# Segment attention on one core: one stretch of 64-row tiles, sums of half 0 in column tiles, value chunks in quarters, dense row copies

## The chip, the core and the metric

One core of a Trainium2 chip runs the whole program. The metric is the device time of one execution in microseconds (us), the median of several runs. Engines are named as in the profile: PE is TensorE (matmul), PEld its weight loads, DVE is VectorE, ACT ScalarE, POOL GpSimd, SP SyncE.

## What is computed

Four layers with residual sums: A, B, A, B, each on the layer norm of the 2048 x 512 input. B is a gated MLP with a 2048 x 2048 spatial matmul and takes little of the time. A is attention with a recurrent memory, and its recurrence sets the order of everything:

```python
B, S, Dm = (1, 2048, 512); H, Dh = (32, 128); M, seg = (8, 32)
mem = mem0
for s in range(n_seg):                                # 64 segments of 32 rows
    h = concatenate([mem, x[:, s * 32:(s + 1) * 32]])  # 8 memory rows + 32 rows
    q, k, v = h @ Wq, h @ Wk, h @ Wv                   # 32 heads of 128
    p = softmax(where(mask, q @ k.T * scale, -1e9))    # 40 x 40 for each head
    o = (p @ v) @ Wo
    mem = o[:, :8]                                     # input of the next segment
    outs.append(o[:, 8:])
```

## The kernel before

**Blocks.** `a_block` runs layer A, `b_block` layer B, each twice. In `a_block` a loop over 64 segments calls `segment`; the order of PE, DVE and ACT is the order in which the program issues them (`manual_schedule`), while the queues of POOL and SP are ordered by the framework. The 32 heads are worked in two halves `r` (0 and 1) of 16 heads.

**Two sorts of rows.** The 32 rows of a segment that it computes at once (24 new rows and the 8 memory rows that the segment before has just made) are `hT`, 32 columns wide. The projections of the last 8 rows of the four segments of a block of 128 rows don't hang on the memory: they are computed ahead for the whole block, by `b_units` (tiles `psb`), and the output projection of such rows is made afterwards, by `y_part` (tiles `pwB`). Both are generators, and `fill()` issues their next few matmuls; a segment calls it three times and gets 4, 8 and 20 matmuls. These matmuls are what PE does while the chain of a segment is in another engine. Some segments have nothing left to fill with.

**A segment, as PE sees it.** `qk(0)`, `qk(2)`, `qk(1)`, `qk(3)` are the chunks of Q (0, 1) and K (2, 3), `v_mm(0)` and `v_mm(1)` those of V: 16 matmuls each (`mm_chunk`, L710: 4 steps `kt` over the 512 input columns, times 4 column tiles of 32 columns, so a chunk of 32 rows fills all 128 partitions). `qk` copies its chunk from PSUM to a bf16 tile `rows` (L920), and `qk_T` turns it with DVE's 32 x 32 transpose into QQ or KA (L923). The element order in `rows` interleaves two heads, so that the transpose can move pairs as one 4-byte word. `scores(r)` are 20 small matmuls (L946, L950) into `psS`; `exps(r)` is their exponential (L955), `close(r)` multiplies by the mask and makes E (L958). E stands in a layout in which the keys of two heads lie in the 64-row halves of the partitions; so what reads E as the moving operand uses tiles of 64 rows and 128 columns: `sums_memory(r)` (L972, the denominators of the memory queries, by a matrix of ones), `pv(r)` (L989, L992, E times V, where `VA` is the copied value chunk, L1034 and L1043), and `sums_tokens` (L981, all other denominators).

**The way out.** `memory_out(r)` turns the denominators into reciprocals (logarithm and exponential on ACT, L1006 and L1007) and writes the 8 memory rows of `uT` (L1008). `wo_pairs` and `wo_rest` (L790, L797) project them with Wo; `fold` and `build_hA` add the parts and transpose the new memory into the next segment's `hT` (L895), which its first `qk` waits for. `tok_out` and `last_out` (L1011, L1014) write the other rows with the reciprocals of `sums_tokens` (L1076, L1079).

**DVE's tail.** After `last_out(1)` DVE runs what is left for the end of a segment: in some segments an addition of finished outputs (L826, or L832 for a first copy), in some a normalisation for layer B (`y_norm`, L245). The next segment's transposes queue behind it.

**PSUM.** `att` holds psQ, then psS, then psT; `attO[0]` psK, then psO[0]; `attO[1]` psO[1]; `accA` and `accB` take turns for chunks, fill and px. `other_bank` tells the framework that two accesses to a tile lie in different banks.

Of the kernel before, what the change touches and what calls it, by code (L numbers as in the profile page):

```python
# [7 lines left out]
BF16 = mybir.dt.bfloat16  # L8
F32 = mybir.dt.float32
ACT = mybir.ActivationFunctionType  # L10
ALU = mybir.AluOpType
# [3 lines left out]
P = 128  # L15
# [48 lines left out]
def _consts(ctx, tc, c, b_sp):  # L64
    nc = tc.nc
    cp = ctx.enter_context(tc.tile_pool(name="consts", bufs=1))
    bsp = cp.tile([P, 16], F32, name="bsp")
    tctx = ExitStack()
    tmp = tctx.enter_context(tc.tile_pool(name="consts_tmp", bufs=1))
    maskf = tmp.tile([P, 224], F32, name="maskf")  # L70
    nc.gpsimd.memset(maskf[:], 1.0)
    fourth = tmp.tile([P, 4, 32], F32, name="fourth")
    nc.gpsimd.memset(fourth[:], 0.0)
    nc.gpsimd.affine_select(out=fourth[:], in_=fourth[:], compare_op=ALU.not_equal, fill=1.0,
                            base=0, pattern=[[-1, 4], [-4, 32]], channel_multiplier=1)
    own = maskf[:, 160:224].rearrange("p (i q) -> p i q", i=4)
    is_own = tmp.tile([P, 4, 1], F32, name="is_own")
    nc.vector.tensor_reduce(out=is_own[:], in_=fourth[:], op=ALU.max, axis=mybir.AxisListType.X)
    nc.vector.tensor_copy(own, is_own[:].to_broadcast([P, 4, 16]))
    for q in range(0, P, 32):  # L80
        blk = maskf[q:q + 32, 0:160].rearrange("p (i q) -> p i q", i=4)[:, :, 8:32]
        nc.gpsimd.affine_select(out=blk, in_=blk, compare_op=ALU.is_ge, fill=0.0, base=8,
                                pattern=[[0, 4], [1, 24]], channel_multiplier=-1)
        last = own[q:q + 32, :, 8:16]
        nc.gpsimd.affine_select(out=last, in_=last, compare_op=ALU.is_ge, fill=0.0, base=0,
                                pattern=[[1, 4], [4, 8]], channel_multiplier=-1)
    maskN = cp.tile([P, 2, 224], BF16, name="maskN")
    nc.vector.memset(maskN[:], 0.0)
    for gs in range(4):
        nc.vector.tensor_copy(maskN[32 * gs:32 * gs + 32, gs % 2, :], maskf[32 * gs:32 * gs + 32, :])  # L90
    ones = cp.tile([P, P], BF16, name="ones")
    nc.vector.memset(ones[:], 1.0)
    bsp_bf = cp.tile([P, 16], BF16, name="bsp_bf")

    def load_bsp():
        nc.vector.memset(bsp_bf[:], 0.0)
        nc.sync.dma_start(bsp_bf[:], b_sp.rearrange("(t p) -> p t", p=P))
        return lambda: nc.vector.tensor_copy(bsp[:], bsp_bf[:])

    c["bsp"], c["load_bsp"] = bsp, load_bsp  # L100
    tctx.close()
    c.update(maskN=maskN, ones=ones)
    return c


# [476 lines left out]
def cols_rhs(w, j, kt, cg):  # L582
    at = 2048 * (j % 2) + 512 * cg
    return w[j // 2][:, kt, at:at + 512]
# [81 lines left out]
def a_block(tc, c, rows, front, MV_in, RS_in, MV_out, RS_out, ahead, wo, S, first):  # L666
# [1 line left out]
    NSEG = S // SEG  # L668
    NB = S // P
    scale = float(DH) ** -0.5  # L670
    maskN, ones = c["maskN"], c["ones"]

    with ExitStack() as ctx:

# [33 lines left out]
        def mm_chunk(ps, lhs, rhs, kts=range(KT)):  # L708

            return [nc.tensor.matmul(ps[32 * cg:32 * cg + 32, :], lhsT=lhs(kt, cg), rhs=rhs(kt, cg), start=(kt == 0), stop=(kt == KT - 1),  # L710
                                     tile_position=(0, 32 * cg)) for kt in kts for cg in range(4)]
# [179 lines left out]
        def build_hA(s, pw, t1):  # L891

            t, at = memT[s % 2], 32 * (s % 4)
            nc.vector.tensor_tensor(out=t[:], in0=pw, in1=t1[:], op=ALU.add)
            nc.vector.transpose(out=rows.hT[s // 4][:, :, at:at + 32], in_=t[:])  # L895

        def store_o(s, pw, t1):

# [4 lines left out]
        def segment(s, fill, spare1, spare2, spare3, tail, loads):  # L903
# [10 lines left out]
            S = segp.tile([P, 2, 224], BF16, name="S", bufs=1)  # L914
            E = segp.tile([P, 2, 2, 224], BF16, name="E", bufs=1)

            def qk(j, ps):
                mms = mm_chunk(ps, lambda kt, cg: hA_cur[:, kt, :], lambda kt, cg: qk_rhs(w, j, kt, cg))
                r = rowp.tile([P, 512], BF16, name="rows", tag="rowsQK", bufs=3)
                return r, mms, nc.scalar.copy(r[:].rearrange("p (n el two) -> p n two el", n=8, two=2), ps.rearrange("p (n two el) -> p n two el", n=8, two=2))  # L920

            def qk_T(j, r):
                nc.vector.transpose(out=(QQ[:, j % 2, :, 0:32] if j < 2 else KA[:, j % 2]).bitcast(F32).rearrange("p n q one -> p n (q one)"), in_=r[:].bitcast(F32))  # L923

            def v_mm(r, ps):
                return mm_chunk(ps, lambda kt, cg: hA_cur[:, kt, :], lambda kt, cg: cols_rhs(w, 4 + r, kt, cg))

            def ends(q):

# [34 lines left out]
            def e_own(e, b):  # L964
                return e[:, :, 160:224].rearrange("p n (i b e) -> p n i b e", i=4, b=2)[:, :, :, b, :]

            def sums_memory(r):

                for k in range(2):
                    for g in range(2):  # L970
                        e = E[64 * g:64 * g + 64, r]
                        nc.tensor.matmul(psO[r][:, g, 320:384], lhsT=ones[64 * g:64 * g + 64, :], rhs=e_own(e, 0) if k else e_all(e, 0, 8),  # L972
                                         start=(k == 0), stop=True, skip_group_check=True)

            def sums_tokens(ps):
# [8 lines left out]
            def pv(r):  # L984

                for i in range(4):
                    for g in range(2):
                        o = psO[r][:, g, 0:320].rearrange("p (s i q) -> p s i q", s=2, i=4)[:, :, i, :]
                        nc.tensor.matmul(o, lhsT=VA[64 * g:64 * g + 64, r, i, :], rhs=E[64 * g:64 * g + 64, r, :, 40 * i:40 * i + 40],  # L989
                                         start=False, stop=True, skip_group_check=True)  # L990
                for g in range(2):
                    nc.tensor.matmul(ends(heads40(psO[r][:, g, 0:320])), lhsT=VX[64 * g:64 * g + 64, j4, r, :],  # L992
                                     rhs=E[64 * g:64 * g + 64, r, :, 160:224], start=False, stop=True, skip_group_check=True)
# [7 lines left out]
            def rview(r, lo, hi):  # L1001
                return Rt[:].rearrange("p g (r n q) -> p r g n q", r=2, q=32)[:, r, :, :, lo:hi]

            def memory_out(r):
                rm = Rm[:, r]
                nc.scalar.activation(out=rm, in_=psO[r][:, :, 320:384], func=ACT.Ln)  # L1006
                nc.scalar.activation(out=rm, in_=rm, func=ACT.Exp, scale=-1.0)  # L1007
                nc.vector.tensor_tensor(out=hview(uT_cur[:], r, 24, 32), in0=oview(r, 0, 8), in1=rm.rearrange("p g (n q) -> p g n q", q=8), op=ALU.mult)  # L1008

            def tok_out(r):  # L1010
                nc.vector.tensor_tensor(out=hview(uT_nxt[:], r, 0, 24), in0=oview(r, 8, 32), in1=rview(r, 0, 24), op=ALU.mult)  # L1011
# [1 line left out]
            def last_out(r):  # L1013
                nc.vector.tensor_tensor(out=hview(oB, r, 8 * (s % 16), 8 * (s % 16) + 8), in0=oview(r, 32, 40), in1=rview(r, 24, 32), op=ALU.mult)  # L1014

            psQ = att.tile([P, 2, 512], F32, name="psQ")
            r0, _, read = qk(0, psQ[:, 0, :])
            r2, mms, _ = qk(2, psQ[:, 1, :])
            other_bank(mms, read)
            qk_T(0, r0)  # L1020
# [2 lines left out]
            qk_T(1, r1)  # L1023
            psK = attO[0].tile([P, 2, 512], F32, name="psK")
            r3, _, read = qk(3, psK[:, 0, :])
            if first and s == 0:
                fill()
            other_bank(v_mm(0, psK[:, 1, :]), read)
            psS = att.tile([P, 2, 512], F32, name="psS")
            scores(0)  # L1030
            expd = exps(0)
            qk_T(3, r3)
            close(0)
            nc.scalar.copy(VA[:, 0].rearrange("p i e -> p (i e)"), psK[:, 1, :])  # L1034
            if j4 == 0 and tb + 1 < NB and not (first and s == 0):
                ln_turn(tb + 1)
            if first and s == 0:
                fill()
            psW = accB.tile([P, 512], F32, name="psV")
            v_mm(1, psW)  # L1040
            other_bank(scores(1), expd)
            exps(1)
            nc.vector.tensor_copy(VA[:, 1].rearrange("p i e -> p (i e)"), psW[:])  # L1043
            close(1)

            psO = [attO[r].tile([P, 2, 512], F32, name="psO") for r in range(2)]
            Rm = segp.tile([P, 2, 2, 64], F32, name="Rm", bufs=1)
            if not (first and s == 0):
                fill()
            sums_memory(0)  # L1050
            pv(0)
            memory_out(0)
            spare1(E)
            if not (first and s == 0):
                fill()
            sums_memory(1)
            pv(1)
            psT = att.tile([P, 2, 512], F32, name="psT")
            sums_tokens(psT)
            memory_out(1)  # L1060
            run(copies)
            if first and s == 0:
                ahead_of_wo()
            px = accB.tile([P, 512], F32, name="px")
            wo_pairs(px, uT_cur)
            pw = psO[0][:, 0, 384:512]
            if first and s == 0:
                wo_rest(pw, uT_cur, hi=wo.low + 8)
                ahead_of_wo()
                wo_rest(pw, uT_cur, lo=wo.low + 8)  # L1070
            else:
                wo_rest(pw, uT_cur)
# [213 lines left out]
```

## Time and profile before

| | |
|---|---|
| runs | 1641.54, 1642.6, 1644.31 us, median 1642.6 |
| profiled execution | 1639.89 us, span 1638.2 us |
| granted clock of PE | 0.998 |
| busy: PE, DVE, ACT, POOL | 1588.3, 1076.4, 1142.0, 292.5 us |
| layers A (starts 29.9 and 841.5 us) | about 654 us each |
| a segment with fill | 10.16 us in most cases |

A busy PE counts the latency of each matmul; as matmuls overlap, the distance of their starts tells more. The timeline merges neighbours of one line: its columns are the start, the time until the last one ends, the engine, line and operation, the tiles and the count. In the groups by form the last columns are the busy time, the mean duration in ns, and the idle time ahead with what ended it.

### The profile page before, as it was taken

The page shows a single profiled execution, that of the slowest core. Times are in us where ns is not written, and L with a number is a line of the kernel's source. Part 1 is how long each engine was busy: PE and PEld are TensorE (multiplying, and loading weights), DVE is VectorE, ACT ScalarE, POOL GpSimd, SP SyncE. Part 2 cuts the span into 40 slices and gives each one's busy share as a digit, 9 for nine tenths or more (in the row PEclk, how much of TensorE's full clock was granted, in tenths as well). Part 3 has the DMA queues.
Part 4 walks back from the last instruction along what each step waited for, and adds up shares of the span by engine and source line. Part 5 has one row for each costly group of instructions (what it writes and reads, how often), then busy time and mean ns, then how long its engine had stood idle before and what let it go on. Part 6 is the DMA issues. An engine that isn't in the chain of part 4 may idle for free.

```text
span 1638.2 us, 87178 instructions
## 1 busy us (share of the span) xinstructions
PE 1588.3 (97%) x39111; PEld 947.5 (58%) x39134; DVE 1076.4 (66%) x2923; ACT 1142.0 (70%) x2281; POOL 292.5 (18%) x604
## 2 busy tenths in 40 slices
PE   5799999999999999999999999999999999999999
PEld 2455655555556556566655555565555566555565
DVE  3566666667776776784466666666677667767722
ACT  3688888888888888760048888888888888876400
POOL 5111111112211212320011111111122112214000
PEclk9999999999999999999999999999999999999999
DMA  9312212112222333278951211122233123335696
GB/s 363 90 42 43 42 45 43 43 42 75 80 56 43 77 86 82 85 189 169 202 156 46 46 45 46 45 46 46 58 91 84 46 58 95 87 74 162 147 199 159
DMA packets 263598, 148.78 MB, mean 91 GB/s; under 512 B 197560, under 2 KB 239648, under 8 KB 263224
## 3 DMA queue, kind: packets, MB, share of 16 engines
q1 hardware_dynamic: 249992, 99.38, 27.3%
q0 software_dynamic: 13232, 43.82, 8.1%
q8 instruction: 307, 5.03, 1.3%
q14 instruction: 67, 0.55, 0.1%
HBM read 59.68 MB, written 37.19 MB: 59 GB/s over the span
## 4 chain that ended last, share of the span: by engine, by line
PE 55%; DVE 1%; issue 0%; DMA 0%; ACT 0%; SPq 0%; DVEq 0%
PE pg L393 9%; PE psQ L710 7%; PE psK L710 7%; PE psb L710 5%; PE pz L292 5%; PE px L790 4%; PE psm L710 3%; PE psV L710 3%; PE psO L797 3%; PE py L436 2%; PE pwB L809 2%; PE psO L972 1%; PE psO L989 1%; PE psT L981 1%; PE psS L946 1%; PE pw L1238 0%
## 5 line engine op out<-in xcount | busy, mean ns | idle before, releaser
L710 PEld LDWEIGHTS <-hT 128*32 128x32 bf16 x12288 | 332.7, 97 | 307.9 <-DVE hT L895 29.2
L920 ACT CAST rows<-psQ 128x512 bf16<-128x512 f32 x256 | 180.8, 758 | 17.1 <-PE psQ L710 12.4
L923 DVE STREAM_TRANSPOSE QQ<-rows 128x256 f32<-128x256 f32 x256 | 113.6, 444 | 99.9 <-ACT rows L920 99.4
L1011 DVE TENSOR_TENSOR uT<-psO,Rt 128x384 bf16<-128x384 f32 x256 | 140.5, 549 | 35.7 <-ACT Rt L1079 34.8
L923 DVE STREAM_TRANSPOSE KA<-rows 128x256 f32<-128x256 f32 x256 | 113.8, 445 | 62.2 <-ACT rows L920 62.1
L393 PE MATMUL pg<-z,wspT 128*128 128x344 bf16 x1024 | 154.3, 309 | 0.0
L1079 ACT ACTIVATE Rt<-Rt 128x512 f32<-128x512 f32 x256 | 147.3, 622 | 4.1
L710 PE MATMUL psQ<-Wq_sb,hT 128*32 128x512 bf16 x2048 | 135.3, 381 | 13.2 <-DVE hT L895 9.0
L1008 DVE TENSOR_TENSOR uT<-psO,Rm 128x128 bf16<-128x128 f32 x256 | 74.7, 292 | 96.0 <-ACT Rm L1007 94.9
L881 POOL COPY KX<-old 128x128 bf16<-128x128 bf16 x128 | 69.3, 541 | 383.4 <-PE psS L950 257.4
L790 PEld LDWEIGHTS <-uT 128*32 128x32 bf16 x4608 | 110.7, 96 | 44.0 <-DVE uT L1008 32.0
L710 PE MATMUL psQ<-Wk_sb,hT 128*32 128x512 bf16 x2048 | 135.2, 381 | 0.0
L710 PE MATMUL psm<-Wq_sb,hT 128*32 128x512 bf16 x2048 | 134.8, 380 | 0.0
L790 PE MATMUL px<-Wo,uT 128*32 128x256 bf16 x3840 | 134.5, 274 | 0.0
L710 PE MATMUL psK<-Wk_sb,hT 128*32 128x512 bf16 x2048 | 134.3, 379 | 0.0
L710 PE MATMUL psK<-Wv_sb,hT 128*32 128x512 bf16 x2048 | 134.3, 379 | 0.0
L710 PE MATMUL psV<-Wv_sb,hT 128*32 128x512 bf16 x2048 | 133.3, 378 | 0.0
L1076 ACT ACTIVATE Rt<-psT 128x1024 f32<-128x1024 f32 x128 | 131.0, 1023 | 3.1
L881 POOL COPY KX<-front 128x128 bf16<-128x128 bf16 x126 | 67.6, 543 | 364.9 <-PE psS L950 253.7
L393 PEld LDWEIGHTS <-wspT 128*128 128x128 bf16 x1024 | 100.2, 98 | 53.2
L797 PE MATMUL psO<-Wo_high,uT 128*32 128x128 bf16 x7168 | 125.2, 219 | 3.1 <-issue 2.8
L955 ACT ACTIVATE S<-psS 128x224 bf16<-128x224 f32 x256 | 91.4, 357 | 52.7 <-PE psS L950 52.2
(195 smaller groups left out, 2922.3 us busy)
## 6 DMA issues: line engine op xcount, KB each, us to landing
o_d<-o_sb SPq DMA_DIRECT2D x126, 64.0 KB
vb_d<-front SPq DMA_DIRECT2D x30, 256.0 KB
VX<-vb_d SPq DMA_DIRECT2D x120, 64.0 KB
ln_x<-xd SPq DMA_DIRECT2D x26, 256.0 KB
y_o<-o_d POOLq DMA_DIRECT2D x22, 256.0 KB, 3.3
xd<-y_o POOLq DMA_DIRECT2D x22, 256.0 KB, 3.1
Wq_sb<-in_A_Wq_dram POOLq DMA_DIRECT2D x8, 512.0 KB, 8.6
Wk_sb<-in_A_Wk_dram POOLq DMA_DIRECT2D x8, 512.0 KB, 10.4
```

Source lines behind the costliest of these rows:

```text
L292: nc.tensor.matmul(pz[:, c0:c1], lhsT=xnT[:, kt, :], rhs=w_in_sb[:, kt, c0:c1], start=(kt == 0), stop=(kt == KT - 1))
L393: nc.tensor.matmul(pg[t][:, k, 0:344], lhsT=wsp[t][:, st, :], rhs=z(st, 344 * k, 344 * k + 344), start=(st == 0), stop=(st == NT - 1))
L710: return [nc.tensor.matmul(ps[32 * cg:32 * cg + 32, :], lhsT=lhs(kt, cg), rhs=rhs(kt, cg), start=(kt == 0), stop=(kt == KT - 1), tile_posi ...
L790: nc.tensor.matmul(px[at:at + 32, 0:256], lhsT=lhs[:, h, :], rhs=wo_rhs(h, slice(k + 2, None, -2) if h % 2 else slice(k, None, 2)), start= ...
L797: nc.tensor.matmul(pw[32 * cg:32 * cg + 32, :], lhsT=lhs[:, h, :], rhs=wo_rhs(h, cg), start=False, stop=(h == H - 1), tile_position=(0, 32 ...
L881: eng.tensor_copy(KX[:, :, r].rearrange("p g (k i) -> p i g k", i=4), bs["KTB"][:, r].rearrange("p (i g) k -> p i g k", i=4)[:, :, :, 8 * ...
L920: return r, mms, nc.scalar.copy(r[:].rearrange("p (n el two) -> p n two el", n=8, two=2), ps.rearrange("p (n two el) -> p n two el", n=8, ...
L923: nc.vector.transpose(out=(QQ[:, j % 2, :, 0:32] if j < 2 else KA[:, j % 2]).bitcast(F32).rearrange("p n q one -> p n (q one)"), in_=r[:]. ...
L955: return nc.scalar.activation(out=S[:, r], in_=psS[:, r, 0:224], func=ACT.Exp, scale=scale)
L1011: nc.vector.tensor_tensor(out=hview(uT_nxt[:], r, 0, 24), in0=oview(r, 8, 32), in1=rview(r, 0, 24), op=ALU.mult)
L1076: nc.scalar.activation(out=Rt[:], in_=psT[:], func=ACT.Ln)
L1079: nc.scalar.activation(out=rt, in_=rt, func=ACT.Exp, scale=-1.0)
```

## The change

`sums_memory(0)` becomes `sums_zero`: a matmul over all 128 rows with 32-column weights (`half`, ones in one half of the rows), in the tile shape of the chunks, into a free part of `psS`. All matmuls with 64-row tiles, those of half 1 too, then stand in one stretch: `pv(0)`, `sums_tokens`, `sums_one`, `pv(1)`. The second fill moves behind it. The value chunks are issued in parts (1 and 3 quarters; 2, 1 and 1), with the scores and `sums_zero` between the parts. The row copies of `qk` walk in the order of their output, so they write densely and read PSUM with a step; that of `qk(0)` goes from ACT to DVE, and the copies of the value chunks change places between ACT and DVE. The reciprocals of half 0 start ahead of `close(1)`. The transpose of the new memory is made in two halves. The accumulator `pw` moves from psO[0] to psO[1].

```diff
+    half = cp.tile([P, 2, 32], BF16, name="half")
+    nc.vector.memset(half[:], 0.0)
+    for g in range(2):
+        nc.vector.memset(half[64 * g:64 * g + 64, g, :], 1.0)
...
-            nc.vector.transpose(out=rows.hT[s // 4][:, :, at:at + 32], in_=t[:])
+            for k in range(2):
+                nc.vector.transpose(out=rows.hT[s // 4][:, 2 * k:2 * k + 2, at:at + 32], in_=t[:, 64 * k:64 * k + 64])
...
-                return r, mms, nc.scalar.copy(r[:].rearrange("p (n el two) -> p n two el", n=8, two=2), ps.rearrange("p (n two el) -> p n two el", n=8, two=2))
+                return r, mms, copy(r[:].rearrange("p (n el two) -> p n el two", n=8, two=2), ps.rearrange("p (n two el) -> p n el two", n=8, two=2))
...
+            def sums_zero(pN):
+
+                return [nc.tensor.matmul(pN[32 * cg:32 * cg + 32, 64 * g:64 * g + 64], lhsT=half[:, g, :], rhs=e_own(E[:, 0], 0) if k else e_all(E[:, 0], 0, 8),
+                                         start=False, stop=True, tile_position=(0, 32 * cg), skip_group_check=True)
+                        for k in range(2) for g in range(2) for cg in range(4)]
...
-                                         start=False, stop=True, skip_group_check=True)
+                                         start=(r == 0 and i == 0), stop=True, skip_group_check=True)
...
-            r0, _, read = qk(0, psQ[:, 0, :])
+            r0, _, read = qk(0, psQ[:, 0, :], nc.vector.tensor_copy)
...
-            other_bank(v_mm(0, psK[:, 1, :]), read)
+            other_bank(v_mm(0, psK[:, 1, :], (0,)), read)
             psS = att.tile([P, 2, 512], F32, name="psS")
             scores(0)
             expd = exps(0)
             qk_T(3, r3)
+            other_bank(v_mm(0, psK[:, 1, :], (1, 2, 3)), read)
             close(0)
-            nc.scalar.copy(VA[:, 0].rearrange("p i e -> p (i e)"), psK[:, 1, :])
+            nc.vector.tensor_copy(VA[:, 0].rearrange("p i e -> p (i e)"), psK[:, 1, :])
...
-            v_mm(1, psW)
+            v_mm(1, psW, (0, 1))
             other_bank(scores(1), expd)
-            exps(1)
-            nc.vector.tensor_copy(VA[:, 1].rearrange("p i e -> p (i e)"), psW[:])
+            expd = exps(1)
+            v_mm(1, psW, (2,))
+            pN = psS[:, 0, 224:352]
+            other_bank(sums_zero(pN), expd)
+            v_mm(1, psW, (3,))
+            Rm = segp.tile([P, 2, 2, 64], F32, name="Rm", bufs=1)
+            invert = inverse(0, pN.rearrange("p (g q) -> p g q", g=2))
+            nc.scalar.copy(VA[:, 1].rearrange("p i e -> p (i e)"), psW[:])
+            invert()
             close(1)
...
-            sums_memory(0)
             pv(0)
+            psT = att.tile([P, 2, 512], F32, name="psT")
+            sums_tokens(psT)
+            sums_one()
+            pv(1)
             memory_out(0)
             spare1(E)
...
                 fill()
-            sums_memory(1)
-            pv(1)
-            psT = att.tile([P, 2, 512], F32, name="psT")
-            sums_tokens(psT)
+            inverse(1, psO[1][:, :, 320:384])()
             memory_out(1)
...
-            pw = psO[0][:, 0, 384:512]
+            pw = psO[1][:, 0, 384:512]
```

`inverse(r, src)` issues the logarithm of `src` and gives back a function that issues the exponential; `sums_one` is `sums_memory` for half 1.

More of the change, by code (lines that the diff above doesn't have):

```diff
@@ L101, in _consts @@
     tctx.close()
-    c.update(maskN=maskN, ones=ones)
+    c.update(maskN=maskN, ones=ones, half=half)
     return c
@@ L670, in a_block @@
     scale = float(DH) ** -0.5
-    maskN, ones = c["maskN"], c["ones"]
+    maskN, ones, half = c["maskN"], c["ones"], c["half"]
     with ExitStack() as ctx:
@@ L915, in segment, with qk, v_mm @@
             E = segp.tile([P, 2, 2, 224], BF16, name="E", bufs=1)
-            def qk(j, ps):
+            def qk(j, ps, copy=nc.scalar.copy):
                 mms = mm_chunk(ps, lambda kt, cg: hA_cur[:, kt, :], lambda kt, cg: qk_rhs(w, j, kt, cg))
                 r = rowp.tile([P, 512], BF16, name="rows", tag="rowsQK", bufs=3)
-                return r, mms, nc.scalar.copy(r[:].rearrange("p (n el two) -> p n two el", n=8, two=2), ps.rearrange("p (n two el) -> p n two el", n=8, two=2))
+                return r, mms, copy(r[:].rearrange("p (n el two) -> p n el two", n=8, two=2), ps.rearrange("p (n two el) -> p n el two", n=8, two=2))
             def qk_T(j, r):
                 nc.vector.transpose(out=(QQ[:, j % 2, :, 0:32] if j < 2 else KA[:, j % 2]).bitcast(F32).rearrange("p n q one -> p n (q one)"), in_=r[:].bitcast(F32))
-            def v_mm(r, ps):
-                return mm_chunk(ps, lambda kt, cg: hA_cur[:, kt, :], lambda kt, cg: cols_rhs(w, 4 + r, kt, cg))
+            def v_mm(r, ps, kts=range(KT)):
+                return mm_chunk(ps, lambda kt, cg: hA_cur[:, kt, :], lambda kt, cg: cols_rhs(w, 4 + r, kt, cg), kts)
             def ends(q):
@@ L965, in e_own, with sums_one @@
                 return e[:, :, 160:224].rearrange("p n (i b e) -> p n i b e", i=4, b=2)[:, :, :, b, :]
-            def sums_memory(r):
+            def sums_zero(pN):
+                return [nc.tensor.matmul(pN[32 * cg:32 * cg + 32, 64 * g:64 * g + 64], lhsT=half[:, g, :], rhs=e_own(E[:, 0], 0) if k else e_all(E[:, 0], 0, 8),
+                                         start=False, stop=True, tile_position=(0, 32 * cg), skip_group_check=True)
+                        for k in range(2) for g in range(2) for cg in range(4)]
+            def sums_one():
                 for k in range(2):
                     for g in range(2):
-                        e = E[64 * g:64 * g + 64, r]
-                        nc.tensor.matmul(psO[r][:, g, 320:384], lhsT=ones[64 * g:64 * g + 64, :], rhs=e_own(e, 0) if k else e_all(e, 0, 8),
+                        e = E[64 * g:64 * g + 64, 1]
+                        nc.tensor.matmul(psO[1][:, g, 320:384], lhsT=ones[64 * g:64 * g + 64, :], rhs=e_own(e, 0) if k else e_all(e, 0, 8),
                                          start=(k == 0), stop=True, skip_group_check=True)
@@ L1002, in rview, with inverse @@
                 return Rt[:].rearrange("p g (r n q) -> p r g n q", r=2, q=32)[:, r, :, :, lo:hi]
+            def inverse(r, src):
+                rm = Rm[:, r]
+                nc.scalar.activation(out=rm, in_=src, func=ACT.Ln)
+                return lambda: nc.scalar.activation(out=rm, in_=rm, func=ACT.Exp, scale=-1.0)
             def memory_out(r):
[L1005 to L1008, printed above, removed]
+                nc.vector.tensor_tensor(out=hview(uT_cur[:], r, 24, 32), in0=oview(r, 0, 8), in1=Rm[:, r].rearrange("p g (n q) -> p g n q", q=8), op=ALU.mult)
             def tok_out(r):
@@ L1014, in last_out @@
                 nc.vector.tensor_tensor(out=hview(oB, r, 8 * (s % 16), 8 * (s % 16) + 8), in0=oview(r, 32, 40), in1=rview(r, 24, 32), op=ALU.mult)
+            begin = first and s == 0
             psQ = att.tile([P, 2, 512], F32, name="psQ")
-            r0, _, read = qk(0, psQ[:, 0, :])
+            r0, _, read = qk(0, psQ[:, 0, :], nc.vector.tensor_copy)
             r2, mms, _ = qk(2, psQ[:, 1, :])
@@ L1025, in segment @@
             r3, _, read = qk(3, psK[:, 0, :])
-            if first and s == 0:
+            if begin:
                 fill()
-            other_bank(v_mm(0, psK[:, 1, :]), read)
+            other_bank(v_mm(0, psK[:, 1, :], (0,)), read)
             psS = att.tile([P, 2, 512], F32, name="psS")
@@ L1032, in segment @@
             qk_T(3, r3)
+            other_bank(v_mm(0, psK[:, 1, :], (1, 2, 3)), read)
             close(0)
-            nc.scalar.copy(VA[:, 0].rearrange("p i e -> p (i e)"), psK[:, 1, :])
-            if j4 == 0 and tb + 1 < NB and not (first and s == 0):
+            nc.vector.tensor_copy(VA[:, 0].rearrange("p i e -> p (i e)"), psK[:, 1, :])
+            if j4 == 0 and tb + 1 < NB and not begin:
                 ln_turn(tb + 1)
-            if first and s == 0:
+            if begin:
                 fill()
             psW = accB.tile([P, 512], F32, name="psV")
-            v_mm(1, psW)
+            v_mm(1, psW, (0, 1))
             other_bank(scores(1), expd)
-            exps(1)
-            nc.vector.tensor_copy(VA[:, 1].rearrange("p i e -> p (i e)"), psW[:])
+            expd = exps(1)
[7 more added lines that the diff above has]
+            invert()
             close(1)
             psO = [attO[r].tile([P, 2, 512], F32, name="psO") for r in range(2)]
-            Rm = segp.tile([P, 2, 2, 64], F32, name="Rm", bufs=1)
-            if not (first and s == 0):
+            if not begin:
                 fill()
-            sums_memory(0)
             pv(0)
+            psT = att.tile([P, 2, 512], F32, name="psT")
+            sums_tokens(psT)
+            sums_one()
+            pv(1)
             memory_out(0)
             spare1(E)
-            if not (first and s == 0):
+            if not begin:
                 fill()
-            sums_memory(1)
-            pv(1)
-            psT = att.tile([P, 2, 512], F32, name="psT")
-            sums_tokens(psT)
+            inverse(1, psO[1][:, :, 320:384])()
             memory_out(1)
             run(copies)
-            if first and s == 0:
+            if begin:
                 ahead_of_wo()
@@ L1065, in segment @@
             wo_pairs(px, uT_cur)
-            pw = psO[0][:, 0, 384:512]
-            if first and s == 0:
+            pw = psO[1][:, 0, 384:512]
+            if begin:
                 wo_rest(pw, uT_cur, hi=wo.low + 8)
```

## The prediction

> **What bounds the kernel now.** I read the page first, then TensorE's timeline of one segment, then the timelines of VectorE (DVE) and ScalarE (ACT) over the same stretch, and last the groups by form for the prices. The page says that TensorE (PE) is never without work:
>
> ```profile
> PE 1588.3 (97%) x39111; PEld 947.5 (58%) x39134; DVE 1076.4 (66%) x2923; ACT 1142.0 (70%) x2281; POOL 292.5 (18%) x604
> ```
>
> Busy is not useful, so I looked at starts. The timeline of PE, second half of the segment that starts at 305.98:
>
> ```profile
> 311.08 0.39 PE L710 MATMUL psV<-Wv_sb,hT 128*32 128x512 bf16 x4
> 311.30 0.27 PE L946 MATMUL psS<-QQ,KA 128*32 128x40 bf16 x16
> 311.40 0.20 PE L950 MATMUL psS<-QQ,KX 128*32 128x64 bf16 x4
> 311.43 0.39 PE L710 MATMUL psb<-Wq_sb,hB 128*32 128x512 bf16 x4
> 311.75 0.23 PE L972 MATMUL psO<-E,ones 64*128 64x64 bf16 x4
> 311.81 0.31 PE L989 MATMUL psO<-E,VA 64*128 64x80 bf16 x8
> 311.96 0.22 PE L992 MATMUL psO<-E,VX 64*128 64x128 bf16 x2
> 312.11 0.61 PE L710 MATMUL psb<-Wq_sb,hB 128*32 128x512 bf16 x8
> 312.65 0.23 PE L972 MATMUL psO<-E,ones 64*128 64x64 bf16 x4
> 312.72 0.31 PE L989 MATMUL psO<-E,VA 64*128 64x80 bf16 x8
> 312.87 0.22 PE L992 MATMUL psO<-E,VX 64*128 64x128 bf16 x2
> 312.92 0.43 PE L981 MATMUL psT<-E,ones 64*128 64x512 bf16 x4
> ```
>
> The second column is latency; throughput is the distance of starts. Four 512-column matmuls in column tiles (a quad, one quarter of a chunk) take 0.216 us. At 311.43 a quad of `psb` is followed by the first 64-row matmul 0.32 later, and at 312.11 two quads (0.43) by the next 64-row matmul 0.54 later: 0.103 too long both times. Leaving, the last L992 pair is followed after 0.150 where inside the stretch it is 0.058: 0.092 too long. I followed all 128 segments by these starts: 0.309 to 0.322 on entry in nearly every segment with fill, whatever data is late. So this is a price of changing from 128x32 to 64x128 tiles, not a wait. 117 segments have fill matmuls and mostly take 10.16 us; ten have none and take 9.91 to 10.14, and these do wait for E and hT.
>
> **What goes and comes on PE.** There are four changes of tile shape in a segment, and two after: minus 0.103 + 0.092 = 0.195. `sums_memory(0)` goes, 311.75 to 311.81: minus 0.069. `sums_zero` comes, 16 matmuls of 64 columns in column tiles; its row is L950, a quad of 64 columns in 0.0295: plus 4 x 0.0295 = 0.118. Quartering the value chunks and moving `sums_tokens` ahead of `pv(1)` keep every matmul: 0. Net -0.146 us a segment, if nothing is late.
>
> **What is late.** Positions are counted from the segment's first `qk` matmul. Half of the old cover is given up: `scores(0)` moves from 4.32 to 3.67 (four chunks of 0.864 and a quad), `scores(1)` from 5.31 to 4.88, `sums_zero` comes at 5.23, `pv(0)` at 5.87, `sums_tokens` at 6.08.
>
> First the row copies, which decide. Rows:
>
> ```profile
> L920 ACT CAST rows<-psQ 128x512 bf16<-128x512 f32 x256 | 180.8, 758 | 17.1 <-PE psQ L710 12.4
> L1043 DVE CAST VA<-psV 128x512 bf16<-128x512 f32 x128 | 88.5, 692 | 2.7
> L1034 ACT CAST VA<-psK 128x512 bf16<-128x512 f32 x128 | 74.3, 580 | 0.0
> L895 DVE STREAM_TRANSPOSE hT<-memT 128x128 bf16<-128x128 bf16 x126 | 39.2, 311 | 6.2
> ```
>
> L920 writes every second bf16 and takes 0.758 where a dense copy of the same size (L1034) takes 0.580. After the change the write is dense, but the PSUM read jumps 32 words at each element. No row shows such a read from PSUM. The nearest is a DVE transpose that reads SBUF so:
>
> ```profile
> L629 DVE STREAM_TRANSPOSE VX<-ln_xn x16: 350/366/410, 38.0 to 836.4; 128x128 bf16<-128x128 bf16 x16
> ```
>
> That is 0.366 against 0.311 for L895: 0.43 ns an element, 0.22 us on 512. So the copy lies between 0.58 and 0.80 on ACT and between 0.69 and 0.91 on DVE. I take the low ends: reads from PSUM in runs of 8 cost nothing (L1008 takes 0.292 with them, L889 0.292 without). [...] A copy shorter than a dense one has no reason in any row.
>
> *scores(0).* Row copy 0 now stands in DVE's queue behind the previous segment's tail. An ordinary tail, and one with an output add (L826):
>
> ```profile
> 317.64 0.28 DVE L1014 TENSOR_TENSOR old<-psO,Rt 128x128 bf16<-128x128 f32 x1
> 318.63 0.45 DVE L923 STREAM_TRANSPOSE QQ<-rows 128x256 f32<-128x256 f32 x1 [0.71 <-ACT rows L920]
> ...
> 328.10 0.68 DVE L826 TENSOR_TENSOR yB<-pwB,yB 128x512 f32<-128x512 f32 x1
> 328.70 0.43 DVE L923 STREAM_TRANSPOSE QQ<-rows 128x256 f32<-128x256 f32 x1
> ```
>
> From the starts 316.14 and 326.40 the tails end at 1.79 and 2.38. The copy begins 0.086 before the tail's end (so do neighbours on DVE), takes 0.692, the dependent transpose follows after 0.034, the second 0.361 later with 0.41, and PE starts 0.055 after it (688.10 to 688.15): tail + 1.47. An ordinary tail gives 3.26, in time for 3.67. With 2.36 PE waits 0.15. By segment, 38 have such a tail (L826, L832 or `y_norm`, L245), and four at the ends of both blocks have 2.95 to 3.7, which costs 0.66 to 1.3 each, 4.1 in all.
>
> *scores(1).* ACT may read chunk 3 at 3.68; 0.58 copy, 0.033 hop, 0.445 transpose, 0.055: 4.79, just ahead of 4.88. This margin of 0.09 is what a slow read would eat.
>
> *E of half 1.* In the old order E starts 0.83 after `scores(1)` and takes 0.38; with the hop, 1.27. Now 1.20 of PE work lies between (scores 0.13, two value quads 0.43, `sums_zero` 0.12, a fill quad with the entry 0.32, `pv(0)` 0.20). PE waits 0.07, with `pv(1)`, the second fill and the output projection queued behind it.
>
> The rest keeps its cover. `VA` of half 0, now on DVE, lands at 5.67: `pv(0)` needs it at 5.82, and E of half 1, queued behind it, has its input at 5.71. `VA` of half 1 goes to ACT (0.58) behind the logarithm of `pN`, done about 6.40; `pv(1)` starts at 6.50. The inverse of half 0 ends at 6.61, its `memory_out` at 6.94, the projection starts at 7.22; half 1 is done by 7.8, its head 16 is due at 8.1. Uncovered, each would cost its own lateness. Two half transposes in place of L895 add 0.1 to DVE ahead of `tok_out`, which waits for ACT anyway; PE is still in fill. No DMA is added, and what SP and POOL issue stands where it stood; POOL's copies for the next segment, which the scores release, start by as much earlier as the scores. Three memsets for `half` lie under the opening weight loads.
>
> **Sum.** 75 ordinary segments: -0.146 + 0.067 = -0.079, -5.9. 38 with a long tail: -0.079 + 0.15, +2.7. The four: +4.1. Ten without fill: one change of shape less and an earlier projection (7.23 to 6.99), a little from the half transposes: -0.28, -2.8. Total -1.9 us. The profiled run took 1639.9 (span 1638.2) and becomes 1638.0; the median of the runs, 1642.6, becomes 1640.7, no change by the 0.2% (3.3 us) that a measurement of this kernel can tell.
>
> **Rivals.**
> *The jumping read costs 0.22 us a copy, as L629 has it.* Place: chunk 3's copy, then `scores(1)`, and copy 0 on DVE. It decides from 0.09 on. Ordinary segments wait 0.13 more (+0.05, +3.8); long tails 0.37 in place of 0.15 (+0.29, +11); the four +5; no fill -1.5. Together +18: 1661, slower. For it: L629. Against: that read is from SBUF and in bf16.
> [...]
> *The two waits are covered after all,* the hops being shorter when queues are empty: without 117 x 0.067 and 38 x 0.15 it is 13.5 less, 1627. Against: the hops were read where the engines stood idle.
> *The drain stays* because `sums_zero` pays it: excluded as far as the rows go, since L950 among chunks shows no gap.
>
> **How the numbers follow.** Free reads 0.58 (own range 1633 to 1648, the long tails and the margin of 0.09 being its unknowns), read penalty 0.22, doubled 0.08, covered 0.12. The first ends as faster, same or slower with 0.26, 0.20, 0.12; the covered case is faster; the others are slower. So faster 0.38, same 0.20, slower 0.42. The range 1626 to 1662 takes in the first and the covered case and half of the read penalty (0.57 + 0.12 + 0.11) and leaves out the doubled one.
>
> **What would show it.** Entries of about 0.31 once, not twice, a segment; `sums_zero` in 0.12; the row copies of ACT at 0.58 and that of DVE at 0.69; a gap of 0.07 in front of `sums_tokens`; `scores(0)` late only behind L826, L832 and L245. I am wrong if the row copies stay at 0.75 or above, if `scores(1)` waits in ordinary segments, or if a segment without late data is not 10.01 to 10.08.

## The result: 10 us slower, and the profile after

The median of four runs is 1652.9 us (1649.9 to 1656.6) beside 1642.8 for the kernel before in the same comparison: the ratio is 1.0068, 95% interval 1.0053 to 1.0084. The profiled execution took 1654.0 (span 1652.3), 14.1 more than the profiled one of before. The forecast was 1640.7 and "no change" at this point; the time lies in the range, but the side is wrong.

The page after, the line of the engines and the line of the row copies (line, engine, operation | busy us, mean ns of one | idle of the engine ahead of them, what ended most of it):

```profile
PE 1589.0 (96%) x40647; PEld 966.1 (58%) x40670; DVE 1151.6 (70%) x3180; ACT 976.7 (59%) x2153; POOL 288.0 (17%) x604
...
L925 ACT CAST rows<-psQ 128x512 bf16<-128x512 f32 x128 | 74.9, 585 | 146.0 <-DVE rows L925 131.5
```

The copies are as fast as the forecast took them to be, 0.585. What is new is the right-hand part: ScalarE (ACT) stood idle for 146 us ahead of its copy of chunk 2, where before the figure was 17.1, for chunks 0 and 2 together, and the releaser was TensorE (PE). Now 131.5 of it was ended by *VectorE's (DVE's) row copy*. No line of the prediction has this wait.

PE's timeline after, second half of the ordinary segment that starts at 294.36:

```profile
299.59 0.28 PE L974 MATMUL psS<-E,half 128*32 128x64 bf16 x16
299.70 0.39 PE L714 MATMUL psV<-Wv_sb,hT 128*32 128x512 bf16 x4
299.92 0.39 PE L714 MATMUL psb<-Wq_sb,hB 128*32 128x512 bf16 x4
300.24 0.32 PE L1000 MATMUL psO<-E,VA 64*128 64x80 bf16 x8
300.39 0.22 PE L1003 MATMUL psO<-E,VX 64*128 64x128 bf16 x2
300.47 0.45 PE L992 MATMUL psT<-E,ones 64*128 64x512 bf16 x4
300.75 0.22 PE L983 MATMUL psO<-E,ones 64*128 64x64 bf16 x4
300.81 0.31 PE L1000 MATMUL psO<-E,VA 64*128 64x80 bf16 x8
300.95 0.22 PE L1003 MATMUL psO<-E,VX 64*128 64x128 bf16 x2
301.11 0.62 PE L714 MATMUL psb<-Wq_sb,hB 128*32 128x512 bf16 x8
```

This is the plan come true. There is one entry into the 64-row tiles (299.92 to 300.24, 0.32 for a quad of 0.216) and one exit (300.95 to 301.11, 0.16); `sums_zero` takes 0.11; ahead of `sums_tokens` there are 0.08, some 0.02 of them a wait. The segment takes 10.03, where it took 10.16.

A segment behind a long DVE tail, starting at 324.70: DVE's timeline, then ACT's over the same stretch, then PE's weight load for `scores(0)` (in brackets the idle time ahead, and what ended it):

```profile
326.41 0.68 DVE L830 TENSOR_TENSOR yB<-pwB,yB 128x512 f32<-128x512 f32 x1
327.00 0.68 DVE L925 CAST rows<-psQ 128x512 bf16<-128x512 f32 x1
327.72 0.45 DVE L928 STREAM_TRANSPOSE QQ<-rows 128x256 f32<-128x256 f32 x1
328.39 0.45 DVE L928 STREAM_TRANSPOSE KA<-rows 128x256 f32<-128x256 f32 x1 [0.23 <-ACT rows L925]
```

```profile
324.41 1.15 ACT L1100 ACTIVATE Rt<-Rt 128x512 f32<-128x512 f32 x2
327.77 0.59 ACT L925 CAST rows<-psQ 128x512 bf16<-128x512 f32 x1 [2.22 <-DVE rows L925]
```

```profile
328.89 0.17 PEld L951 LDWEIGHTS <-KA 128*32 128x32 bf16 x16 [0.84 <-DVE KA L928]
```

ACT was free from 0.86 of the segment on (325.56), and chunk 2 could have been read from 1.95 on (that is where its copy begins in two experiments below). Still the copy began only at 3.07 of the segment (327.77), after DVE had ended its copy of chunk 0. So the steps are serial: copy 0 on DVE, then copy 2 on ACT, then the transpose of `KA`. `scores(0)` starts at tail + 1.81, which is 4.19, where PE is free for it at 3.67. This segment takes 10.75, and the median of its kind is 10.56.

Where the 14.1 us of the two profiled executions went, over all segments: 38 with a long tail (in the changed kernel it ends later than 2.2 of the segment) +15.6; the other 84 inside the blocks -11.9; the segments at the block ends, with what follows the last two of each block, +7.5 (1.9, 1.4, 1.3, 2.9); the first segment of the first block +1.4 and of the second +1.5. The medians lie only 10.1 apart: the profiled execution of before is 2.9 under its median, the changed one 1.1 over, so single terms of this list hold for these two executions.

### The profile page after: what moved, and what is told of

Read it like the earlier page. It is cut to its first block, busy times and chain, and to the rows that moved or that the text cites. A ratio compares the mean times of both kernels' runs of the same rounds, so it can differ in the third digit from the quotient of the medians.

```text
span 1652.3 us, 90089 instructions
## 1 busy us (share of the span) xinstructions
PE 1589.0 (96%) x40647; PEld 966.1 (58%) x40670; DVE 1151.6 (70%) x3180; ACT 976.7 (59%) x2153; POOL 288.0 (17%) x604
## 4 chain that ended last, share of the span: by engine, by line
PE 49%; DVE 4%; ACT 4%; issue 1%; DMA 0%; ACTq 0%; DVEq 0%
PE pg L397 9%; PE psK L714 5%; PE psQ L714 5%; PE psb L714 5%; PE pz L296 5%; PE px L794 4%; PE psV L714 3%; PE psm L714 2%; PE psO L801 2%; PE py L440 2%; PE psO L1000 1%; ACT rows L925 1%; DVE uT L1024 1%; PE psT L992 1%; ACT Rt L1097 1%; PE psS L951 1%
## 5 line engine op out<-in xcount | busy, mean ns | idle before, releaser
L714 PE MATMUL psV<-Wv_sb,hT 128*32 128x512 bf16 x2048 | 165.3, 379 | 0.0
L925 ACT CAST rows<-psQ 128x512 bf16<-128x512 f32 x128 | 74.9, 585 | 146.0 <-DVE rows L925 131.5
L714 PE MATMUL psK<-Wv_sb,hT 128*32 128x512 bf16 x2048 | 153.9, 378 | 0.0
L794 PEld LDWEIGHTS <-uT 128*32 128x32 bf16 x4608 | 122.7, 97 | 33.4 <-DVE uT L1021 3.6
```

Of the source, the lines that this page charges most:

```text
L794: nc.tensor.matmul(px[at:at + 32, 0:256], lhsT=lhs[:, h, :], rhs=wo_rhs(h, slice(k + 2, None, -2) if h % 2 else slice(k, None, 2)), start= ...
L925: return r, mms, copy(r[:].rearrange("p (n el two) -> p n el two", n=8, two=2), ps.rearrange("p (n two el) -> p n el two", n=8, two=2))
```

## The experiments

Theory T: the loss is an order between two reads. Copies 0 and 2 read the two banks of one PSUM tile, `psQ`. While both were on ACT they needed no order (before: 17.1 us of idle ahead of the copies, 12.4 of it ended by PE and none by a row copy); on two engines the program makes one wait for the other (131.5 us). It costs where the DVE tail is late. Rivals: D, the place of copy 0 behind the tail alone; J, the jumping PSUM read; S, the new order of work on PE; A, ACT as the new bound. Each kernel was compared with runs of the kernel before on the same chip.

**e1_no_order: the one order taken away.**

```diff
-            r2, mms, _ = qk(2, psQ[:, 1, :])
+            r2, mms, read2 = qk(2, psQ[:, 1, :])
             other_bank(mms, read)
+            other_bank([read2], read)
```

> The changed kernel, with the one order between ScalarE's copy of chunk 2 (bank 1 of psQ) and VectorE's copy of chunk 0 (bank 0) declared away; nothing else. Theory T (the loss is this order: the two copies of one PSUM tile go one after the other, so scores(0) starts at tail + 1.81 instead of + 1.47): ScalarE's idle in front of L925 falls from 146 us to under 30; scores(0) behind a long VectorE tail comes at 3.85 instead of 4.19 of the segment, 38 x 0.33 + 9 x 0.14 + 4 x 0.34 = 15 us less: 1638 us, ratio to the kernel before 0.997. Rival D (the loss is the place of copy 0 in VectorE's queue behind the tail, and the order behind it costs nothing): 1653, ratio 1.006. Rival J (the copies read PSUM in jumps and are slow for it): no change either.

Measured 1634.4 (1633.7 to 1637.1), ratio 0.996, interval 0.9945 to 0.9975. The answer on the line of the row copies, on both engines, names what ended the idle time ahead of them (us, times):

```profile
  PE psQ L714: 51.9, 52
  PE psK L714: 34.0, 122
  PE psm L714: 29.5, 102
  DVE QQ L928: 5.5, 6
```

DVE's row copy is gone as a releaser; what is left for `psQ` is waiting for PE's data (49.9 on ACT, more than the 30 expected), and six copies waited for a transpose. The same segment as above, now from 321.44, on DVE, on ACT and at PE's weight load:

```profile
323.14 0.68 DVE L830 TENSOR_TENSOR yB<-pwB,yB 128x512 f32<-128x512 f32 x1
323.74 0.68 DVE L925 CAST rows<-psQ 128x512 bf16<-128x512 f32 x1
324.45 0.45 DVE L928 STREAM_TRANSPOSE QQ<-rows 128x256 f32<-128x256 f32 x1
324.82 0.41 DVE L928 STREAM_TRANSPOSE KA<-rows 128x256 f32<-128x256 f32 x1
```

```profile
323.39 0.58 ACT L925 CAST rows<-psQ 128x512 bf16<-128x512 f32 x1 [1.09 <-PE psQ L714]
```

```profile
325.28 0.17 PEld L951 LDWEIGHTS <-KA 128*32 128x32 bf16 x16 [0.50 <-DVE KA L928]
```

ACT now copies chunk 2 beside DVE's work, and `KA` follows `QQ` by 0.37. `scores(0)` starts at 3.84, within 0.01 of the prediction's tail + 1.47, and the median of the 38 segments is 10.21 instead of 10.56. T holds and D falls: one dependency between two reads was worth about 18 us against the changed kernel's 1652.9, somewhat more than the 15 expected. J falls with it, since the read still jumps. S falls too: PE's new order stands, and the kernel is a little faster than before.

**e2_row0_act: copy 0 back on ACT.**

```diff
-            r0, _, read = qk(0, psQ[:, 0, :], nc.vector.tensor_copy)
+            r0, _, read = qk(0, psQ[:, 0, :])
```

> The changed kernel with the copy of chunk 0 back on ScalarE, all four copies dense as in the change. T: no copy waits for another engine, and behind a long tail VectorE has only the two transposes left: scores(0) ready at 2.38 + 0.90 = 3.28, before 3.67. 38 x 0.5 + 4 x 1.0 + 9 x 0.14 = 24 us less; where ScalarE itself ends late (the copies of psb and the square root of RS at its tail, until 2.24) scores(0) comes 0.1 late, some 30 segments, +3: 1632, ratio 0.993. Rival D: as T in the sign, since it takes the copy out of that queue, but only the 0.69 of the copy: the same. Rival J: 1653. Rival A (ScalarE becomes the bound with its fourth copy): 1655 or more.

Measured 1629.3 (1625.7 to 1631.0), ratio 0.9923, interval 0.9908 to 0.9937. Most long tails wait for nothing (`scores(0)` at 3.67 in the median). Rival A falls: ACT carries four copies in this order.

**e3_row0_split: copy 0 on the engine that is free.**

```diff
+        late = [False]
...
         def y_norm(tb, store):
+            late[0] = True
...
-            r0, _, read = qk(0, psQ[:, 0, :], nc.vector.tensor_copy)
+            r0, _, read = qk(0, psQ[:, 0, :], nc.scalar.copy if late[0] else nc.vector.tensor_copy)
...
+            if not late[0]:
+                other_bank([read2], read)
...
+            late[0] = bool(adds)
             run(adds)
```

> The changed kernel; copy 0 goes to ScalarE in the segments behind a VectorE tail that holds an output add or y_norm, and stays on VectorE in all others, there without the order between the copies of chunks 0 and 2. T: no segment waits for scores(0) but the four at the block ends, which win 1.0 each: 1653 - 38 x 0.5 - 4 - 9 x 0.14 = 1628, ratio 0.991, faster than both kernels. Rival A (ScalarE ends late in the same segments): half of it, 1640.

Measured 1626.3 (1624.5 to 1630.1), ratio 0.9904, interval 0.9887 to 0.992: faster than both kernels, 26.6 us under the change as given. The same segment, from 323.24, on ACT and on DVE:

```profile
324.33 0.59 ACT L927 CAST rows<-psQ 128x512 bf16<-128x512 f32 x1 [0.23 <-PE psQ L714]
325.19 0.59 ACT L927 CAST rows<-psQ 128x512 bf16<-128x512 f32 x1 [0.28 <-PE psQ L714]
```

```profile
324.95 0.68 DVE L830 TENSOR_TENSOR yB<-pwB,yB 128x512 f32<-128x512 f32 x1
325.55 0.44 DVE L930 STREAM_TRANSPOSE QQ<-rows 128x256 f32<-128x256 f32 x1
325.91 0.40 DVE L930 STREAM_TRANSPOSE KA<-rows 128x256 f32<-128x256 f32 x1
```

Copy 0 is done while DVE is still at its tail, and copy 2 ends at 325.78, 0.15 behind the tail, under the `QQ` transpose. So the tail is followed by the transposes alone, and PE finds `scores(0)` ready. It is little ahead of e2; their intervals overlap.

**e5_before_dense_dve: the copies of the change in the old order of PE.**

```diff
-            def qk(j, ps):
+            def qk(j, ps, copy=nc.scalar.copy):
...
-                return r, mms, nc.scalar.copy(r[:].rearrange("p (n el two) -> p n two el", n=8, two=2), ps.rearrange("p (n two el) -> p n two el", n=8, two=2))
+                return r, mms, copy(r[:].rearrange("p (n el two) -> p n el two", n=8, two=2), ps.rearrange("p (n two el) -> p n el two", n=8, two=2))
...
-            r0, _, read = qk(0, psQ[:, 0, :])
+            r0, _, read = qk(0, psQ[:, 0, :], nc.vector.tensor_copy)
```

> The kernel before, with one part of the change alone: dense row copies, that of chunk 0 on VectorE (PE's order, the two stretches and the places of scores and sums stay as before). T: the same wait stands on ScalarE (over 100 us of idle in front of the row copies), but scores(0) is due at 4.32 and comes at 4.19 behind a long tail, so only the four segments at the block ends lose, some 0.7 each: 1645, ratio 1.002. Rival J (the copies themselves are what costs): 1655 or more. Rival S (the loss comes from the new order on PE, not from the copies): 1642, no change.

Measured 1647.2 (1645.5 to 1647.9), ratio 1.0031, interval 1.0018 to 1.0044. The line of the page:

```profile
L920 ACT CAST rows<-psQ 128x512 bf16<-128x512 f32 x128 | 75.1, 587 | 144.6 <-DVE rows L920 132.1
```

The same wait, to the microsecond. But here PE reaches `scores(0)` at 4.32 and finds it ready: the 38 segments take 10.16 as before, and the block ends lose 5.3 in all (`scores(0)` at 4.86 to 5.69 there); the first segment of the second block is 1.7 longer, as in the changed kernel (see below). The wait came with the copies, its price behind the other long tails with the earlier scores.

**e4_before_dense: dense copies alone, all on ACT, in the old order of PE.** The diff is that of e5 without its last pair of lines.

> The kernel before with its row copies dense, all four still on ScalarE; no order on PE changed. T: the copies fall from 0.758 to 0.585, but nothing waits for them in the old order (scores(0) is due at 4.32): 1641.5, ratio 1.000. With the run of row copies all on ScalarE in the new order (1629) this gives the worth of the rest of the change, one stretch and the moved sums: 12 us. Rival C (the dense copies alone win, since ScalarE is in the chain of waits): some 0.1 a segment, 1630.

Measured 1640.5 (1636.4 to 1647.6), ratio 1.000, interval 0.9986 to 1.0014: nothing, as T says. The same copies in the new order (e2) stand at 0.9923, so the rest of the change, taken together (the one stretch, the moved sums, the value copies and what else moved), is worth 0.8% when no row copy is late.

**e7_strided: e2 with the old, strided copies.**

```diff
-                return r, mms, copy(r[:].rearrange("p (n el two) -> p n el two", n=8, two=2), ps.rearrange("p (n two el) -> p n el two", n=8, two=2))
+                return r, mms, copy(r[:].rearrange("p (n el two) -> p n two el", n=8, two=2), ps.rearrange("p (n two el) -> p n two el", n=8, two=2))
```

> The changed kernel with all four row copies on ScalarE and in the old form: dense read, write of every second bf16 (0.758 each). T, by the prediction's own numbers: chunk 3 may be read at 3.68, + 0.758 + 0.033 + 0.445 + 0.055 = 4.97, so scores(1), due at 4.88, is 0.09 late in the 117 segments with fill: +10 on the 1629 of the dense form, 1639. Rival N (the margin is larger than I took it, and dense copies are worth nothing here): 1629. Rival Q (the four copies queue up, chunk 1 and 3 wait for ScalarE too): 1650 or more.

Measured 1642.8 (1640.9 to 1646.5), ratio 1.0013, interval 1.0003 to 1.0023: 13.6 us over e2, where 10 were expected. The line of the page:

```profile
L925 ACT CAST rows<-psQ 128x512 bf16<-128x512 f32 x256 | 180.8, 758 | 16.3 <-PE psQ L714 12.1
```

`scores(1)` starts at 4.97 in the median, and at 4.88 in e2: the forecast's figures. Dense copies are worth nothing in the old order and the whole gain in the new one.

**e8_two_stretches: e3 with the second fill inside the stretch.**

```diff
             sums_tokens(psT)
+            if not begin:
+                fill()
             sums_one()
             pv(1)
             memory_out(0)
             spare1(E)
-            if not begin:
-                fill()
```

> The kernel with copy 0 split, and the second fill moved from behind pv(1) to between sums_tokens and sums_one: the same work, one more exit and entry of the 64-row tiles. T (a change of tile shape in and out costs 0.103 + 0.092): +0.195 in 117 segments with fill, 22.8 us: 1649, ratio 1.005; where the fill covers PE's wait for E or VA of half 1 it is up to 0.03 less, 1645. Rival W (the stretch as such costs nothing, what was won was waiting): 1626.

Measured 1674.1 (1672.6 to 1675.1), ratio 1.0199, interval 1.0182 to 1.0216: 48 us more, twice what was expected. PE's timeline:

```profile
1093.24 0.45 PE L994 MATMUL psT<-E,ones 64*128 64x512 bf16 x4
1093.61 0.61 PE L714 MATMUL psb<-Wq_sb,hB 128*32 128x512 bf16 x8
1094.16 0.23 PE L985 MATMUL psO<-E,ones 64*128 64x64 bf16 x4
1094.23 0.31 PE L1002 MATMUL psO<-E,VA 64*128 64x80 bf16 x8
1094.37 0.22 PE L1005 MATMUL psO<-E,VX 64*128 64x128 bf16 x2
1094.52 1.05 PE L794 MATMUL px<-Wo,uT 128*32 128x256 bf16 x30
1095.30 0.62 PE L794 MATMUL px<-Wo_high,uT 128*32 128x256 bf16 x6
```

`sums_tokens` takes 0.37 up to the fill instead of 0.28, and two quads of fill 0.55 instead of 0.43. By ordinary segments the projection starts 0.20 later than in e3 (7.39 and 7.19): that is the extra change of shape, 0.195 in the forecast. A further 0.25 falls behind that start (projection to the next segment 3.09, and 2.84 in e3): the fill no longer covers the inverse of half 1, and head 16 waits for it (`Wo_high` follows `Wo` by 0.78 in both, but its six matmuls take 0.45 instead of 0.21). I had left this out of the expectation. That part is read from the trace, not tested by itself.

**e6_split_sums64: e3 with the memory sums of half 0 back in 64-row tiles, inside the stretch.** `sums_zero` and its place beside the scores go; `sums_memory(0)`, as before the change, stands ahead of `pv(0)`, and the inverse of half 0 behind it.

```diff
-            other_bank(sums_zero(pN), expd)
...
+            sums_memory(0)
             pv(0)
+            inverse(0, psO[0][:, :, 320:384])()
```

> The kernel with copy 0 split between ScalarE and VectorE, and the memory sums of half 0 back as four 64-row matmuls, now inside the one stretch ahead of pv(0): 0.118 of sums_zero goes, 0.069 comes. T: 0.049 less on PE in each of 128 segments, 6 us: 1620, ratio 0.987, provided that the inverse of half 0 (two ScalarE steps of 0.3 from 6.15 on) and memory_out(0) end by 7.0, ahead of the projection at 7.14. Rival P (they end later and the projection waits for them 0.1): 1633.

Measured 1629.0 (1628.6 to 1630.2), ratio 0.9927, interval 0.9912 to 0.9942: no gain over e3, where 6 us were expected. `pv(0)` does start 0.05 earlier (5.83), but `sums_tokens` stays at 6.11, which is when E of half 1 comes, and the projection starts 0.05 later (7.24) behind the inverse of half 0. So `sums_zero`, dearer on PE, is covered by the wait for E and is the better place.

## Why the prediction was wrong

*Changes of shape and sums: right.* Entry and exit came once instead of twice, the row of `sums_zero` is 0.11 (0.118), and ordinary segments fell by 0.13 where none waited for `scores(0)`. The prediction had 0.08: its wait ahead of `sums_tokens`, 0.07, was some 0.02, so for this wait the rival with the shorter hops was nearer. Ten segments without fill fell by 0.25 in the median (0.28).

*Row copies: right.* The jumping read is free on both engines, 0.585 on ACT and 0.68 on DVE, beside 0.580 and 0.692 for the dense copies L1034 and L1043 of before. The two cases that made it dear, with 0.30 between them, fall. The row that stood behind the penalty of 0.22, L629, reads bf16 from SBUF in jumps of 128 elements inside a transpose, and says nothing of this read. No run shows the doubled copy, to which the chances gave 0.08, nor the 1648 at which the range of the case with free reads ends: the copies took 0.585 and 0.68, and e7, with copies of 0.758 all on ACT, ran 1642.8.

*scores(1): right.* 4.88 with dense copies and 4.97 with strided ones, both measured as forecast.

***scores(0)*: this step failed.** Tail + 1.47 let the `KA` transpose follow `QQ` by 0.361, as it does when copy 2 is long done. The sum has no term for copy 2, and did not ask whether it waits for copy 0, now on the other engine. It does: 0.34 more, so that a long tail costs 0.52 and not 0.15, and a tail of 2.0 costs 0.14 and not nothing. On 38 segments that is +15.6 where +2.7 was forecast, and at the block ends +7.5 for +4.1. With the order away (e1) the 38 segments cost +2.0 against before and the block ends +5.0, near the sum's own terms: there the mechanism as written was sound, and one wait was missing from it. The profiled run of e1 took 1634.0 where the sum said 1638.0; most of the difference is the other 84 segments, -14.8 where -8.7 was forecast.

That the time lies in the range is luck. Of the 0.42 for slower, 0.30 stood on dear reads, and the upper end of 1662 took in half of the read penalty; neither came. In the case with free reads, which did come, the prediction gave slower 0.12.

The kernel before shows the hint: it declares that the *matmuls* of chunk 2 need not wait for the read of chunk 0, since they are in another bank. So the order was made for the tile as a whole here, and a second reader on another engine needed the same declaration. e1 is without this order, and the copies keep their 0.585 and 0.68.

*What no term held.* The first segment of the second block lost 1.5 us to the clock in the profiled run. The windows of one microsecond from its start, in the changed kernel and then before (busy of PE, PEld, DVE, ACT, POOL, then the granted clock, DMA share, GB/s):

```profile
850.06:851.06 1.00, 1.00 (x20) 0.58 (x24) 0.77 (x2) 0.16 (x1) 0.25 (x1) 0.91 0.46 170
851.06:852.06 1.00, 1.00 (x16) 0.48 (x12) 0.78 (x2) 0.34 (x2) 0.00 (x0) 0.50 0.85 291
852.06:853.06 1.00, 1.00 (x13) 0.38 (x8) 0.36 (x1) 0.10 (x1) 0.00 (x0) 0.50 0.44 160
853.06:854.06 1.00, 1.00 (x16) 0.50 (x12) 0.45 (x1) 0.48 (x1) 0.00 (x0) 0.50 0.00 0
854.06:855.06 1.00, 1.00 (x24) 0.51 (x20) 0.00 (x0) 0.49 (x1) 0.00 (x0) 0.88 0.00 0
```

```profile
841.58:842.58 1.00, 1.00 (x20) 0.59 (x24) 0.76 (x2) 0.17 (x1) 0.25 (x1) 1.00 0.27 104
842.58:843.58 1.00, 1.00 (x28) 0.55 (x20) 0.00 (x0) 0.97 (x4) 0.00 (x0) 1.00 0.79 256
```

The first segment of all took 21.9 to 25.2 in the ten profiles, with no pattern that follows an edit, so its +1.4 is left open.

## What to carry to other kernels

When a read of a tile moves to another engine, look for every other reader of that tile: where order is made by tile, as here, two reads that stood in one engine's queue become a chain over two engines, even in different banks. Price an added wait at the place where the consumer now stands, not where it stood: e5 and the change hold the same 132 us of waiting, and one ends 6 us over before, its long-tail segments untouched, and the other loses 0.4 in each of these. And give a moved step to the engine that is free at that moment, segment by segment if the program is written out (e3), rather than to one engine for all.

## What was not expected of the hardware

The PSUM read in jumps of 32 words cost no more than a dense one (0.585 beside 0.580 on ACT, 0.68 beside 0.69 on DVE), while the bf16 write to every second place of SBUF cost 0.17 on 512 elements (0.758 beside 0.585).

After an idle time of PE of 2.42 to 2.48 us ahead of the second block, the granted clock fell to 0.50 in eight of the ten profiles, beginning between the restart and 1.3 us after it (in e7 it was low already at the restart); by the windows the lost clock adds up to 1.5 to 1.7 full microseconds each time, 3.0 to 3.4 us at half rate. In before and e4 it stayed at 1.00 after the same idle time (2.45 and 2.46).

The traces also show what goes with the two cases. In the changed kernel and in before, all records of the granted clock but the final one are 3.413 us long or a whole multiple of it (1, 3, 239, 1 and 234 times; 2, 2 and 470 times), so their borders lie on a grid. In the changed kernel the fall came at a border, at 850.88, and PE had been idle for 0.72 of the 3.413 us ahead of it; in the six others that fell after the restart this share was 0.63 to 0.73. In before the idle time lay over a border, at 839.80, with 0.20 and 0.52 of a window on its two sides. In these two traces, from the first record on, no window of the grid at full clock with PE idle for 0.45 of it or less was followed by a fall; of the five with 0.50 to 0.52, one was (0.504, at 21.44 in the changed kernel); the two inside the span with more, 0.77 (at 24.02 in before) and 0.72, both were. So the loss seems to hang on where the grid stands when the second block begins, which differs from profile to profile. No run shifted the idle time to test it.
